# Dividing by the softmax sums behind the value product in the first three units of an attention and two-MLP kernel

## The chip, the cores and the metric

The kernel runs on one core of a Trainium2 chip. The metric is the device time of one execution in microseconds (us); the kernel before takes 991.06 us (median of three runs, 991.04 to 992.08). Engines are named as in the profile: PE is the matrix engine (TensorE), PEld its weight loads, DVE the vector engine, ACT the scalar engine, POOL is GpSimd, SP issues most transfers.

## What is computed

Three stages follow one another. The change is in the first; the inputs are 64-bit floats in memory, and the kernel works in 32-bit floats, with operands of large products split into a high and a low part (`xh`, `xl`).

```python
# attention: 4 batches, 8 heads, 576 positions, 64 wide, window of 128
scores = scale * q @ k.T                      # per batch and head
scores = where(mask, scores + bias, -1e9)     # ALiBi slope per head, causal window
attn = exp(scores - max(scores))
attn = attn / (sum(attn) + 1e-9)
x = attn @ v                                  # -> 2304 tokens x 512
# gated MLP
y = (silu(x @ w_gate) * (x @ w_val)) @ w_out
# second MLP
h = y @ w_in
out = (h * cos(h)) @ w_out2
```

## The kernel before

Attention works in 16 **units** `u`: a batch and a pair of heads, `NP` = 4 pairs to a batch, so units 0 to 3 are batch 0. A unit has nine **items** `(u, h, i)`: for each head four blocks of 128 rows (`i < NB`), and one tail item (`i == NB`) with the last 64 rows of both heads. Items go in groups of two, and the tail is a group by itself. The groups are called g0 (head 0, blocks 0 and 1), g2 (head 1, blocks 0 and 1), g4 and g6 (blocks 2 and 3 of the two heads) and the tail here.

A loop at line 635 makes one **step** for each item, and each engine's queue holds what the steps issued, in that order; nothing is reordered later. For a group the stages are: scores on PE into one of two `s` banks (`do_s`, issued two groups ahead), bias and row minimum on DVE (`do_bias`, L478), exponential with row sum on ACT (`do_exp`, L487), guard and reciprocal of the sums on DVE (`do_guard` L493, `do_recip` L498), the division on POOL (`do_norm`, L511), transposes on PE (`do_t`, L530; `folded` units 4 and later L520), a copy of the transposed block to SBUF on ACT (`do_hi`, L548, for the tail L543), and, once per unit, the product with the values on PE (`do_pv`, L584, for the tail L562 and L564). The end of `do_pv` is put off to the next step: ACT copies the high part (`xh`, L589, tail L571), DVE subtracts for the low part (`xl`, L590, tail L573). `staged` says how many steps behind a group its transposes, copies and value product come: 5, 6 and 8 (tail 9) in most units, 4, 5 and 6 in the last pair of a batch.

Beside this the loop prepares the next unit's queries and keys (`prep_t` on PE L407, `prep_q` on DVE L413, `prep_k` on ACT L416), and converts nine **pieces** of the first weights (`convert`): two ACT operations (L126, L128), three on DVE (L129, L136, L137), an addition (on POOL L146 for even pieces, on DVE L141 for odd ones), a high part (ACT L168 for even, POOL L173 for odd pieces) and a low part (POOL L161). The tail's value product takes the bank `pq` that the next unit's query transposes use, except in unit 3 of a batch (bank `pm`).

When a batch's last tail has ended (`release`), `filler` may run: dense matmuls of the first MLP (L81 to L83) between the attention's steps. Before batch 0 is through there is none.

Of the kernel before, what the change touches and what calls it, by code (L numbers as in the profile page):

```python
# [9 lines left out]
F32 = mybir.dt.float32  # L10
# [18 lines left out]
def kernel(  # L29
# [12 lines left out]
    nc = tc.nc  # L42
# [56 lines left out]

    def convert(dst, todo, fast=False, act=False):  # L100
# [13 lines left out]
        for i, (key, src, f, column, pool) in enumerate(todo):  # L114
# [19 lines left out]
            if wide:  # L134
# [5 lines left out]
                if fast or (act and i % 2):  # L140
                    nc.vector.tensor_tensor(out=ti, in0=ti, in1=r, op=ALU.add)  # L141
                    added.add(i)
                    yield
                else:
                    def add(i=i, ti=ti, r=r):
                        nc.gpsimd.tensor_tensor(out=ti, in0=ti, in1=r, op=ALU.add)  # L146
                        added.add(i)
                    pool_bg.append((1.25, add))
# [21 lines left out]
            if act and i % 2 == 0:  # L170
# [230 lines left out]
    ptt = const.tile([128, 256], F32, name="ptt")  # L401
    QT, KT, PQ = {}, {}, {}
# [42 lines left out]

    def do_s(groups):
# [3 lines left out]
        for g in groups:  # L450
# [4 lines left out]
            for m, n in enumerate(g):  # L455
# [10 lines left out]
                ST[n] = st, m  # L466
# [5 lines left out]
    def do_bias(n):  # L472
# [4 lines left out]
        st, m = ST[n]  # L477
# [6 lines left out]
    def do_exp(n):  # L484
        w = width(items[n][2])
        e, (st, m) = E[n], ST[n]
        nc.scalar.activation(out=e[:, :w], in_=e[:, :w], func=AF.Exp, bias=st[:, m:m + 1], scale=-1.0,  # L487
                             accum_out=st[:, 2 + 2 * m:3 + 2 * m])

    def do_guard(g):  # L490
        st = ST[g[0]][0]
        c = 2 * len(g) - 1
        nc.vector.tensor_scalar(st[:, 5:5 + c], st[:, 2:2 + c], 1e-9, None, ALU.add)  # L493

    def do_recip(g):
        st = ST[g[0]][0]
        c = 2 * len(g) - 1
# [7 lines left out]
    def do_norm(n):  # L505
        w = width(items[n][2])
        (st, m), e = ST.pop(n), E[n]
# [46 lines left out]

    def do_pv(n):
        u, h, i = items[n]
        b_, p = divmod(u, NP)
        if i == NB:
            vt = nat["v", u]
            ps = (pm.tile([128, 512], F32, tag="pm", name="pm") if u == NP - 1 else  # L560
# [26 lines left out]
        def fin():  # L587
            tok = slice(b_ * S, b_ * S + NB * 128)
            nc.scalar.copy(out=xh[:, p, tok], in_=ps)  # L589
# [36 lines left out]
    def last_pair(n):  # L626

        return 0 <= n < N and items[n][0] == NP - 1

    def staged(n, late, early):  # L630

        if last_pair(n - early) and n - early in final:
            return final[n - early]
        return None if last_pair(n - late) else final.get(n - late)
    for n in range(N + PVS + 2):
# [11 lines left out]
        turned, high = staged(n, TRANS, 4), staged(n, HIGH, 5)  # L647
# [22 lines left out]
        for back in (PVS + 1, PVS, PVS - 2):  # L670
            for m in (ended(back) or ())[-1:]:
                u_, h_, i_ = items[m]
                if (h_ == 1 and i_ == NB - 1 or i_ == NB) and back == (
                        PVS - 2 if last_pair(m) else PVS if i_ == NB - 1 else PVS + 1):
                    do_pv(m)
# [567 lines left out]
```

## Time and profile before

| | |
|---|---|
| median of three runs | 991.06 us |
| the profiled execution's own time | 991.6 us |
| its span, first to last instruction | 989.9 us |
| PE busy | 966.7 us, 98% of the span |
| DVE, ACT, POOL busy | 738.8, 594.0, 479.5 us |
| first bias (L478) of units 0, 1, 2, 3, 4 | 10.34, 21.99, 34.42, 46.99, 60.68 us |
| first filler matmul (L81) | 69.60 us |

[...] A table by form gives a line's instructions of one shape with count, sum and mean, and the idle time before them. A timeline row gives start, length, engine, line and operation, and in brackets the idle time before it with what ended it.

### The profile page before, as it was taken

Reading aid. Unit: us, or ns where it says so; the run is one execution under the profiler, and the core shown is the slowest. Engines: PE = TensorE matmul, PEld = TensorE weight load, DVE = VectorE, ACT = ScalarE, POOL = GpSimd, SP = SyncE. Lnnn points to the kernel's source line nnn. Section 1 sums busy time; section 2 is a strip of 40 time slices with the busy share of each in tenths; the row PEclk is TensorE's granted clock in tenths of the full one; section 3 lists DMA queues with packets and bytes.
Section 4 is the critical chain, followed back from the end, with each engine's and each line's share of the span. In section 5 each row is a group of like instructions: output and inputs, shape, how many; then the busy total and the mean of one; then the engine's idle time right before and its main releaser. Section 6 shows DMA issues by size and latency. Waiting matters only on the chain.

```text
span 989.9 us, 17035 instructions
## 1 busy us (share of the span) xinstructions
PE 966.7 (98%) x5616; PEld 885.2 (89%) x5616; DVE 738.8 (75%) x1552; ACT 594.0 (60%) x1365; POOL 479.5 (48%) x563
## 2 busy tenths in 40 slices
PE   6789999999999999999999999999999999999998
PEld 4468888889999999999999999888989898898886
DVE  6867777766288989989989755889666796666664
ACT  6976666643254545555455433877677776776663
POOL 5756556642245767769678720344222442223221
PEclk9979999999999999999999999999999999999999
DMA  7541333322373637547557625765667656576552
GB/s 181 157 111 45 97 95 74 73 59 91 112 277 107 203 128 235 191 139 249 166 172 243 198 87 167 285 200 185 241 200 230 198 164 198 187 241 201 160 179 85
DMA packets 145159, 163.65 MB, mean 165 GB/s; under 512 B 64688, under 2 KB 105648, under 8 KB 144816
## 3 DMA queue, kind: packets, MB, share of 16 engines
q1 hardware_dynamic: 143872, 162.27, 52.2%
q8 instruction: 45, 0.74, 0.3%
q10 hardware_dynamic: 1200, 0.30, 0.1%
q14 instruction: 42, 0.34, 0.1%
HBM read 126.88 MB, written 35.65 MB: 164 GB/s over the span
## 4 chain that ended last, share of the span: by engine, by line
PE 89%; DVE 3%; ACT 2%; DMA 2%; issue 2%; POOL 1%; SPq 0%; POOLq 0%; DVEq 0%; ACTq 0%
PE l L81 13%; PE l L83 13%; PE l L82 13%; PE pm L81 8%; PE pm L83 8%; PE pm L82 8%; PE pm L966 6%; PE pm L968 5%; PE pm L967 5%; PE s L470 4%; PE pv L584 3%; PE pq L407 1%; PE t L530 1%; PE t L520 1%; POOL e L511 1%
## 5 line engine op out<-in xcount | busy, mean ns | idle before, releaser
L1091 POOL TENSOR_TENSOR r<-r,c 128x384 f32<-128x384 f32 x96 | 104.4, 1089 | 261.7 <-ACT r L1089 172.9
L81 PE MATMUL pm<-xh,wh 128*128 128x384 f32 (+1 forms) x452 | 151.7, 336 | 0.2 <-DVE fu L254 0.2
L83 PE MATMUL pm<-xh,wl 128*128 128x384 f32 (+1 forms) x452 | 144.8, 320 | 0.0
L82 PE MATMUL pm<-xl,wh 128*128 128x384 f32 (+1 forms) x452 | 144.7, 320 | 0.0
L81 PE MATMUL l<-wo,hh 128*128 128x512 f32 x288 | 113.9, 395 | 0.0
L82 PE MATMUL l<-wo,hh 128*128 128x512 f32 x288 | 113.5, 394 | 0.0
L83 PE MATMUL l<-wo,hl 128*128 128x512 f32 x288 | 113.5, 394 | 0.0
L966 PE MATMUL pm<-xh,ws 128*128 128x384 f32 x318 | 107.7, 339 | 0.5 <-ACT q L1117 0.5
L787 POOL TENSOR_TENSOR cs<-cs,st 128x512 uint32<-128x512 uint32 x56 | 80.6, 1439 | 56.5 <-DVE cs L785 47.1
L968 PE MATMUL pm<-xh,ws 128*128 128x384 f32 x318 | 107.6, 338 | 0.0
L967 PE MATMUL pm<-xl,ws 128*128 128x384 f32 x318 | 107.1, 337 | 0.0
L511 POOL TENSOR_SCALAR e<-e,st 128x128 f32<-128x128 f32 (+1 forms) x144 | 60.9, 426 | 58.5 <-DVE st L498 43.7
L81 PEld LDWEIGHTS pm<-xh,wh 128*128 128x128 f32 x452 | 85.1, 188 | 4.0 <-issue 3.0
L82 PEld LDWEIGHTS pm<-xl,wh 128*128 128x128 f32 x452 | 85.3, 189 | 0.0
L83 PEld LDWEIGHTS pm<-xh,wl 128*128 128x128 f32 x452 | 85.0, 188 | 0.0
L1081 ACT ACTIVATE a<-c 128x384 f32<-128x384 f32 x96 | 49.7, 518 | 54.5 <-DVE c L1107 54.5
L487 ACT ACTIVATE e<-e,st 128x256 f32<-128x256 f32 (+1 forms) x144 | 68.0, 474 | 19.0 <-DVE st L478 13.6
L1086 DVE SCALAR_TENSOR_TENSOR r<-a,r 128x384 f32<-128x384 f32 x96 | 76.0, 792 | 3.3
L1088 ACT ACTIVATE r<-r 128x384 f32<-128x384 f32 x96 | 50.3, 524 | 42.7 <-DVE r L1086 42.7
L81 PE MATMUL l<-uh,wh 128*128 128x384 f32 x216 | 72.8, 337 | 0.1
L83 PE MATMUL l<-uh,wl 128*128 128x384 f32 x216 | 72.6, 336 | 0.0
L82 PE MATMUL l<-ul,wh 128*128 128x384 f32 x216 | 72.5, 336 | 0.0
(178 smaller groups left out, 2618.3 us busy)
## 6 DMA issues: line engine op xcount, KB each, us to landing
ws<-wid SPq DMA_DIRECT2D x168, 256.0 KB, 2.8
wo<-wod SPq DMA_DIRECT2D x48, 512.0 KB, 4.9
st<-in_moe_w_out_dram SPq DMA_DIRECT2D x28, 512.0 KB, 3.7
st<-in_moe_w_in_dram SPq DMA_DIRECT2D x16, 512.0 KB, 3.7
st<-in_moe_w_gate_dram SPq DMA_DIRECT2D x12, 512.0 KB, 4.0
st<-in_moe_w_val_dram SPq DMA_DIRECT2D x12, 512.0 KB, 4.0
wid<-sh SPq DMA_DIRECT2D x24, 256.0 KB, 4.2
wid<-sl SPq DMA_DIRECT2D x24, 256.0 KB, 4.0
```

Source lines behind the costliest of these rows:

```text
L81: nc.tensor.matmul(out=ps, lhsT=ah, rhs=bh, start=start, stop=False)
L82: nc.tensor.matmul(out=ps, lhsT=ah, rhs=bl, start=False, stop=False)
L83: nc.tensor.matmul(out=ps, lhsT=al, rhs=bh, start=False, stop=stop)
L487: nc.scalar.activation(out=e[:, :w], in_=e[:, :w], func=AF.Exp, bias=st[:, m:m + 1], scale=-1.0, accum_out=st[:, 2 + 2 * m:3 + 2 * m])
L511: nc.gpsimd.tensor_scalar(e[:, :w], e[:, :w], st[:, 8 + 2 * m:9 + 2 * m], 1.0, ALU.mult, ALU.mult)
L787: nc.gpsimd.tensor_tensor(out=ti, in0=ti, in1=st[:, :, 0], op=ALU.add)
L966: nc.tensor.matmul(out=o, lhsT=wh, rhs=xh_, start=start and kk == 0, stop=False, skip_group_check=True)
L967: nc.tensor.matmul(out=o, lhsT=wh, rhs=xl_, start=False, stop=False, skip_group_check=True)
L968: nc.tensor.matmul(out=o, lhsT=wl, rhs=xh_, start=False, stop=kk == 1, skip_group_check=True)
L1086: nc.vector.scalar_tensor_tensor(out=r, in0=a, scalar=-C2, in1=r, op0=ALU.mult, op1=ALU.add)
L1088: nc.scalar.activation(out=r, in_=r, func=AF.Abs)
L1091: nc.gpsimd.tensor_tensor(out=r, in0=r, in1=h, op=ALU.mult)
```

## The change

In units 0 to 2 the eight row-block items are no longer divided before their transposes (`late`). Their sums are gathered in one tile per unit (`ustats`); after g6 DVE adds the guard and takes the reciprocals once for all eight columns. PE transposes the eight columns into a row tile (`do_row`), DVE copies it to SBUF (`rt`), and PE spreads it over 128 partitions by four products with a constant 0/1 tile (`do_spread`, `pick`). After the value product DVE copies the spread reciprocals to SBUF and multiplies the product by them; POOL then makes the high and the low part. `pick` is set up by two more POOL operations at the start.

The steps behind a group become 3, 4 and 5 in units 0 to 2 (tail 4, 5 and 6), and 4, 5 and 6 in unit 3 (`lag`). The tail's value product of units 0 to 3 takes bank `pm`. For pieces 0 to 5 of the weights, POOL makes all additions and all high parts (`POOLED`).

```diff
+    POOLED = 6
-                if fast or (act and i % 2):
+                if fast or (act and i % 2 and i >= POOLED):
                     nc.vector.tensor_tensor(out=ti, in0=ti, in1=r, op=ALU.add)
-            if act and i % 2 == 0:
+            if act and i % 2 == 0 and i >= POOLED:
                 pool_bg.append((0.0, lambda high=high: post.append(high)))
+    def late(n):
+        u, _, i = items[n]
+        return u < NP - 1 and i < NB
-                ST[n] = st, m
+                ST[n] = (ustats[u], h * NB + i, 8 + h * NB + i) if late(n) else (st, m, 2 + 2 * m)
     def do_guard(g):
         st = ST[g[0]][0]
+        if late(g[0]):
+            if items[g[-1]][1:] == (1, NB - 1):
+                nc.vector.tensor_scalar(st[:, 16:24], st[:, 8:16], 1e-9, None, ALU.add)
+            return
     def do_recip(g):
+        if late(g[0]):
+            if items[g[-1]][1:] == (1, NB - 1):
+                nc.vector.reciprocal(out=st[:, 24:32], in_=st[:, 16:24])
+            return
     def do_norm(n):
+        if late(n):
+            return
+    def do_row(u):
+        RB[u] = pm.tile([128, 512], F32, tag="pm", name="pm")
+        nc.tensor.transpose(RB[u][0:8, 0:128], ustats[u][:, 24:32], ident)
+        post.append(lambda: nc.vector.tensor_copy(out=rt, in_=RB[u][0:8, 0:128]))
+    def do_spread(u):
+        for i in range(NB):
+            nc.tensor.matmul(out=RB[u][:, i * 128:(i + 1) * 128], lhsT=pick[:, i].rearrange("s x c -> s (x c)"),
+                             rhs=rt, start=True, stop=True)
     def do_pv(n):
-            ps = (pm.tile([128, 512], F32, tag="pm", name="pm") if u == NP - 1 else
+            ps = (pm.tile([128, 512], F32, tag="pm", name="pm") if u < NP else
         def fin():
+            if late(n):
+                x = fill_p.tile([128, F0, HT], F32, tag="fu", name="fu").rearrange("p f t -> p (f t)")[:, :NB * 128]
+                by = fill_p.tile([128, F0, HT], F32R, tag="fh", name="fh").rearrange("p f t -> p (f t)")[:, :NB * 128]
+                nc.vector.tensor_copy(out=f32(by), in_=RB.pop(u))
+                nc.vector.tensor_tensor(out=x, in0=ps, in1=f32(by), op=ALU.mult)
+                pool_bg.append((0.6, lambda: nc.gpsimd.tensor_scalar(xh[:, p, tok], x, 1.0, 0.0, ALU.mult, ALU.add)))
+                pool_bg.append((1.25, lambda: nc.gpsimd.tensor_tensor(
+                    out=xl[:, p, tok], in0=x, in1=f32(xh[:, p, tok]), op=ALU.subtract)))
+                return
+    def lag(n):
+        u, _, i = items[n]
+        if u < NP - 1:
+            return (3, 4, 5) if i < NB else (4, 5, 6)
+        return (4, 5, 6) if u == NP - 1 else (TRANS, HIGH, PVS + (i == NB))
```

How the queues stand then is shown at three places. The first is PE, from the first scores of unit 2 (`s<-kx,qx`) on; `t` are transposes, `pv` the value product of unit 1, `pq` the transposes of unit 3's queries. Before:

```order
L470 MATMUL s<-kx,qx 128x128 x2
L470 MATMUL s<-kx,qx 128x256 x2
L530 MATMUL t<-ident,e 128x128 x4
L407 MATMUL pq<-ident,q 128x128 x4
L530 MATMUL t<-ident,e 128x128 x4
L470 MATMUL s<-kx,qx 128x256 x4
L530 MATMUL t<-ident,e 128x128 x2
L419 MATMUL t<-ident,qkt 128x128
L407 MATMUL pq<-ident,k 128x128 x4
L530 MATMUL t<-ident,e 128x128 x3
L584 MATMUL pv<-pth_485,v 64x256
```

The same place in the changed kernel:

```order
L483 MATMUL s<-kx,qx 128x128 x2
L483 MATMUL s<-kx,qx 128x256 x2
L553 MATMUL t<-ident,e 128x128 x4
L583 MATMUL pm<-ident,us_202 8x128
L415 MATMUL pq<-ident,q 128x128 x4
L553 MATMUL t<-ident,e 128x128 x2
L588 MATMUL pm<-rt,pick 128x128 x4
L620 MATMUL pv<-pth_456,v 64x256
...
L483 MATMUL s<-kx,qx 128x256 x4
L553 MATMUL t<-ident,e 128x128 x3
```

The tail's transposes (`x2`), the spread and the whole value product of the unit before now stand ahead of the scores of g4 and g6 (`128x256 x4`) and of the first transposes of the new unit (`x3`).

The second place is DVE, in unit 1, from the bias of the last group but the tail to the tail (before: g6 on; after: the end of g4 on). `xl<-..., xh 64x64` is the low part of the tail of unit 0. Before:

```order
L478 ISA e,st_166<-s,rel 128x256
L478 ISA st_166 128x1
L493 TENSOR_SCALAR st_173<-st_173 128x3
L498 RECIPROCAL st_173<-st_173 128x3
L478 ISA e,st_167<-s,relt,slope 128x192
L478 ISA st_167 128x1
L590 TENSOR_TENSOR xl<-pv,xh 128x512
L129 TENSOR_SCALAR ct<-ct 128x512
L493 TENSOR_SCALAR st_166<-st_166 128x3
L498 RECIPROCAL st_166<-st_166 128x3
L573 TENSOR_TENSOR xl<-pq,xh 64x64 x2
L136 TENSOR_SCALAR ct<-ct 128x512
```

In the changed kernel:

```order
L491 ISA e,us_202<-s,rel 128x256
L491 ISA us_202 128x1
L609 TENSOR_TENSOR xl<-pm,xh 64x64 x2
L131 TENSOR_SCALAR ct<-ct 128x512
L491 ISA e,us_202<-s,rel 128x256
L491 ISA us_202 128x1
...
L138 TENSOR_SCALAR ct<-ct 128x512
L139 SCALAR_TENSOR_TENSOR ct<-st,ct 128x512
L491 ISA e,st_167<-s,relt,slope 128x192
L491 ISA st_167 128x1
L507 TENSOR_SCALAR us_202<-us_202 128x8
L516 RECIPROCAL us_202<-us_202 128x8
```

The tail's low part stood behind the biases of g6 and of the tail; it now stands ahead of both, and two operations of a weight piece (L138, L139) stand between them.

The third place is POOL in unit 3, from the division of g4 (`x2`) to that of the tail (`128x192`). Before:

```order
L511 TENSOR_SCALAR e<-e,st_167 128x256 x2
L173 TENSOR_SCALAR wh<-ct 128x512
L161 TENSOR_TENSOR wl<-ct,wh 128x512
L511 TENSOR_SCALAR e<-e,st_168 128x256 x2
L511 TENSOR_SCALAR e<-e,st_169 128x192
L146 TENSOR_TENSOR ct<-ct,st 128x512
```

In the changed kernel, from the parts of unit 2's product on:

```order
L630 TENSOR_SCALAR xh<-fu 128x512
L631 TENSOR_TENSOR xl<-fu,xh 128x512
L534 TENSOR_SCALAR e<-e,st_167 128x256 x2
L148 TENSOR_TENSOR ct<-ct,st 128x512
L534 TENSOR_SCALAR e<-e,st_168 128x256 x2
L534 TENSOR_SCALAR e<-e,st_169 128x192
```

The addition of the last piece (L148) has moved from behind the last divisions of batch 0 to a place ahead of two of them.

## Rows read from the trace of the kernel before

**Rows 1.** Windows: units 1, 2, 3, batch 0's end, and a stretch behind it.

```profile
21.99:34.42 12.43, 10.17 (x69) 6.51 (x67) 10.72 (x41) 11.32 (x35) 10.22 (x15) 1.00 0.53 136
34.42:46.99 12.57, 9.33 (x63) 6.03 (x63) 10.88 (x39) 11.41 (x35) 9.32 (x13) 1.00 0.64 171
46.99:60.68 13.69, 11.89 (x63) 7.91 (x63) 11.01 (x40) 11.40 (x35) 8.94 (x13) 0.75 0.48 122
60.68:69.57 8.89, 7.31 (x37) 4.44 (x37) 3.99 (x20) 4.18 (x14) 5.26 (x9) 0.62 0.21 48
80.00:90.00 10.00, 10.00 (x82) 8.78 (x82) 7.18 (x34) 6.28 (x24) 7.20 (x16) 1.00 0.21 47
```

**Rows 2.** Table by form, DVE in unit 2.

```profile
L493 DVE TENSOR_SCALAR st<-st 128x3 f32<-128x3 f32 x4 | 1.3, 317 | 0.5 <-ACT e L487 0.5
L129 DVE TENSOR_SCALAR ct<-ct 128x512 f32<-128x512 f32 x2 | 1.2, 592 | 0.0
L413 DVE TENSOR_SCALAR qx<-pq,qscale 128x512 f32<-128x512 f32 x1 | 0.7, 722 | 0.0
L498 DVE RECIPROCAL st<-st 128x3 f32<-128x3 f32 x4 | 0.7, 176 | 0.1
L590 DVE TENSOR_TENSOR xl<-pv,xh 128x512 fp32r<-128x512 f32 x1 | 0.7, 692 | 0.0
L141 DVE CUSTOM_DVE_ANT_0 ct<-st,ct 128x1024 uint16<-128x1024 uint16 x1 | 0.7, 659 | 0.0
```

**Rows 3.** The same table, ACT in unit 2.

```profile
L589 ACT CAST xh<-pv 128x512 fp32r<-128x512 f32 x1 | 0.6, 591 | 0.0
```

**Rows 4.** The same table, POOL in unit 2.

```profile
L511 POOL TENSOR_SCALAR e<-e,st 128x256 f32<-128x256 f32 x6 | 3.2, 547 | 0.5 <-DVE st L498 0.5
L161 POOL TENSOR_TENSOR wl<-ct,wh 128x512 fp32r<-128x512 f32 x2 | 2.5, 1274 | 0.7 <-ACT wh L168 0.6
L146 POOL TENSOR_TENSOR ct<-ct,st 128x512 uint32<-128x512 uint32 x1 | 1.3, 1298 | 0.0
L173 POOL TENSOR_SCALAR wh<-ct 128x512 fp32r<-128x512 f32 x1 | 0.8, 787 | 0.0
```

**Rows 5.** Timeline, PE: single groups of matmuls.

```profile
45.72 0.63 PE L407 MATMUL pq<-ident,q 128*128 128x128 f32 x4 [1.59 <-issue]
38.77 1.73 PE L584 MATMUL pv<-pth,v 128*64 128x256 f32 x16
62.88 2.08 PE L470 MATMUL s<-kx,qx 64*128 64x256 f32 x8
65.29 3.25 PE L584 MATMUL pv<-pth,v 128*64 128x256 f32 x16
```

**Rows 6.** Windows over runs of DVE's (first two) and ACT's work.

```profile
40.97:42.38 1.41, 0.96 (x7) 0.72 (x7) 1.38 (x10) 1.41 (x5) 0.93 (x3) 1.00 1.01 228
45.16:47.85 2.69, 1.36 (x9) 1.00 (x10) 2.54 (x11) 1.65 (x6) 1.26 (x3) 1.00 0.57 198
...
39.04:40.92 1.88, 1.88 (x18) 1.16 (x14) 1.85 (x7) 1.83 (x9) 1.47 (x2) 1.00 1.00 319
43.79:45.15 1.36, 0.34 (x4) 0.10 (x1) 0.35 (x2) 1.33 (x6) 1.28 (x2) 1.00 0.83 189
```

**Rows 7.** Timeline: a guard on DVE and a low part on POOL.

```profile
38.96 1.28 POOL L161 TENSOR_TENSOR wl<-ct,wh 128x512 fp32r<-128x512 f32 x1 [0.61 <-ACT wh L168]
39.49 0.77 DVE L493 TENSOR_SCALAR st<-st 128x3 f32<-128x3 f32 x1
```

**Rows 8.** Windows: three pauses of PE, and the stretch behind one.

```profile
31.50:35.10 3.60, 1.24 (x9) 0.84 (x8) 2.60 (x11) 2.53 (x9) 2.35 (x3) 1.00 0.72 199
44.20:47.90 3.70, 1.41 (x9) 1.05 (x10) 2.71 (x12) 2.63 (x10) 2.22 (x3) 1.00 0.60 186
48.00:54.70 6.70, 6.70 (x28) 4.24 (x28) 6.36 (x23) 6.34 (x20) 5.21 (x7) 0.50 0.59 156
57.90:61.60 3.70, 1.68 (x12) 0.96 (x10) 2.85 (x14) 2.65 (x11) 0.94 (x2) 1.00 0.75 170
```

More of the change, by code (lines that the diff above doesn't have):

```diff
@@ L401 @@
     ptt = const.tile([128, 256], F32, name="ptt")
+    ustats = [const.tile([128, 32], F32, name=f"us{j}") for j in range(NP - 1)]
+    rt = const.tile([8, 128], F32, name="rt")
+    pick = const.tile([8, NB, 2, 64], F32, name="pick")
+    nc.gpsimd.memset(pick, 0.0)
+    nc.gpsimd.affine_select(out=pick, in_=pick, pattern=[[-1, NB], [-NB, 2], [0, 64]], compare_op=ALU.not_equal,
+                            fill=1.0, base=0, channel_multiplier=1)
     QT, KT, PQ = {}, {}, {}
@@ L476, in do_bias @@
         e = e_p.tile([128, 256], F32, tag="e", name="e")
-        st, m = ST[n]
+        st, m, _ = ST[n]
         nc.vector.tensor_tensor_reduce(
@@ L485, in do_exp @@
         w = width(items[n][2])
-        e, (st, m) = E[n], ST[n]
+        e, (st, m, c) = E[n], ST[n]
         nc.scalar.activation(out=e[:, :w], in_=e[:, :w], func=AF.Exp, bias=st[:, m:m + 1], scale=-1.0,
-                             accum_out=st[:, 2 + 2 * m:3 + 2 * m])
+                             accum_out=st[:, c:c + 1])
     def do_guard(g):
         st = ST[g[0]][0]
+        if late(g[0]):
+            if items[g[-1]][1:] == (1, NB - 1):
+                nc.vector.tensor_scalar(st[:, 16:24], st[:, 8:16], 1e-9, None, ALU.add)
+            return
         c = 2 * len(g) - 1
@@ L506, in do_norm @@
         w = width(items[n][2])
-        (st, m), e = ST.pop(n), E[n]
+        (st, m, _), e = ST.pop(n), E[n]
+        if late(n):
+            return
         if folded(n) and w == 256:
@@ L553, in do_hi @@
                                     in1=mold, op=ALU.mult)
+    RB = {}
+    def do_row(u):
[6 more added lines that the diff above has]
+                             rhs=rt, start=True, stop=True)
     def do_pv(n):
@@ L624, with staged @@
     due = pdue = 0.0
[L626 to L634, printed above, removed]
+    def lag(n):
[3 more added lines that the diff above has]
+        return (4, 5, 6) if u == NP - 1 else (TRANS, HIGH, PVS + (i == NB))
+    def staged(n, stage):
+        for j in range(3, PVS + 2):
+            if n - j in final and lag(n - j)[stage] == j:
+                return final[n - j]
+        return None
     for n in range(N + PVS + 2):
@@ L646 @@
             do_s([first[u * NI + j] for j in AHEAD[idx]])
-        turned, high = staged(n, TRANS, 4), staged(n, HIGH, 5)
+        turned, high = staged(n, 0), staged(n, 1)
         if high:
@@ L669 @@
         due += 0.3 * RATE
[L670 to L675, printed above, removed]
+        valued = staged(n, 2)
+        if turned and items[turned[-1]][1:] == (1, NB - 1) and late(turned[-1]):
+            do_row(items[turned[-1]][0])
+        if valued and (items[valued[-1]][1:] == (1, NB - 1) or items[valued[-1]][2] == NB):
+            if late(valued[-1]):
+                do_spread(items[valued[-1]][0])
+            do_pv(valued[-1])
         if v1 is not None:
```

## The prediction

> **What bounds the kernel now.** I read the windows first [rows 1]. From about 70 us on PE is busy without a break (10.00 of 10 us from 80 to 90), so what happens there is fixed PE work, whose order the change leaves alone. Time can be won or lost only in batch 0, before the filler starts at 69.60 us; from then on every microsecond gained or lost goes straight to the end. Batch 0 runs in periods, one per unit: 12.43, 12.57 and 13.69 us for units 1 to 3, and 8.89 us from unit 4's first bias to the filler [rows 1]. In a period ACT works 11.3 to 11.4 us, DVE 10.7 to 11.0, POOL 8.9 to 10.2. No engine is full: ACT waits about 1 us for DVE's biases and DVE 1.5 to 2.7 us for ACT and PE. Two busy engines hand a chain to and fro, so the sums of work alone don't say what a period will be; the order of the queues counts as well.
>
> The second thing to see is PE's clock. It stands at 1.00 over units 1 and 2, at 0.75 on average over unit 3 and at 0.62 over the end [rows 1]. [...] Once low it stays so for 6.7 us of full PE work [rows 8]. The value product takes 3.25 us at the low level and 1.73 us at the high one, eight score matmuls 2.08 us at the low one, so some 1.04 at the high [rows 5].
>
> **The work, part by part, for each of units 0 to 2.** DVE loses three of its guards (0.32 us each), three reciprocals (0.18), one piece's addition (0.66) and the low part of the product (0.69): 2.85 us. It gains the copy of the spread reciprocals, which I price by the query copy, also from a PSUM bank and 512 wide (0.72), the product with them, priced by the low part, which reads the same two memories (0.69), and the row copy, for which I take a guard's 0.3: 1.7 us. Net -1.1 us [rows 2]. ACT loses the high part of the product (0.59) and one piece's high part, a cast of the same shape: -1.2 us [rows 3]. POOL loses eight divisions of about 0.55 us, 4.4 us, and gains 0.79 + 1.27 for the product's parts and 1.30 + 0.79 for a piece: 4.15 us [rows 4]; it stays as it is. PE gains four small products, like four query transposes (0.63), and one transpose of 8 columns, at most a quarter of that: 0.8 us [rows 5]. The wait of the query transposes for the tail's bank (1.59 us [rows 5]) goes away with the move to `pm`; but PE is not what a period waits for there, and I count nothing for it. The two set-up operations of `pick` run on POOL while the first inputs are still being loaded: nothing. By these sums a period would shrink by 1.1 to 1.2 us. That is the first rival. I don't forecast it, because of the order.
>
> **The loop of a period after the change.** I follow units 1 and 2 from DVE's low part of a tail around to the next one, in the queue order shown with the change. On DVE stand the tail's low part, a piece's L129 operation, the bias of g6, the piece's two others, the tail's bias, guard and reciprocal, the first bias of the next unit, and the tail's own guard and reciprocal. The rows of before hold the same operations in two runs, 1.41 and 2.69 us [rows 6], without the L129 one, 0.59 [rows 2]: 4.7 us. Then POOL divides the tail, 0.55 at most [rows 4]. Then PE, in order: the tail's transposes (0.4, from four in 0.63), the spread (0.63), the value product (1.73), the scores of g4 and g6 (1.04), the first transposes (0.5): 4.3 us [rows 5]. Only then can ACT copy the first transposed block, and its queue is in order too: behind that copy come the next queries' tail, a piece's L128 operation, the exponentials of g4, and only then the tail's high part, for which DVE's low part waits. The same operations take 1.88 and 1.36 us [rows 6]: 3.2 us. Sum 4.7 + 0.55 + 4.3 + 3.2 = 12.8 us. The work got less by 1.1 us, but the value product and the spread have come into the chain, and the tail's low part, which stood behind the biases of g6 and the tail, now holds both up. So a period is 12.8 us in place of 12.43 and 12.57: +0.6 us for units 1 and 2 together. Bounds: -1.1 each (the sums), +1.0 each.
>
> [...] A guard on three elements took 0.77 us where others take far less, and it ended within 0.02 us of the end of POOL's low part beside it [rows 7]. [...]
>
> **The start.** Up to unit 1's first bias DVE loses three guards and three reciprocals, 1.5 us at the means, and the addition of piece 1, 0.66 [rows 2]: 2.1 us at most. The piece's next operations still wait for their load and for ACT, so I take -1.6. Bounds: 0 and -2.1.
>
> **The clock.** At the end of unit 1 the score matmuls of unit 2 need the bank that the bias of g6 frees, and then the one that the tail's bias frees. Between these stand two DVE operations of a piece, and ahead of the first stands the wait for ACT. In my walk PE has, between the tail's scores and the second of these banks, 4.4 us with only the transposes of g4 (0.63) and one or two score matmuls, about 0.8 us of work. That is a longer and emptier pause than the two behind which the clock fell and the one behind which it did not [rows 8]. So I expect a fall to 0.50 there, near 32 us, which the kernel before doesn't have. It hits the PE part of the loop, which is now in the chain: at the low level throughout, its 4.3 us become 8.2, +3.9; if PE is low only in front of the value product, +1.3. I take +2.6 for unit 2. Bounds: 0 and +3.9.
>
> **Unit 3 and the end.** Unit 3 keeps its divisions on POOL, and ran with the low clock before as well [rows 8]. DVE gets the row copy, the copy and the multiplication of unit 2 for one low part: +1.0 us by the prices above, and I take +0.9. Bounds: -1.1 (no fall there: 13.69 becomes unit 2's 12.57 [rows 1]) and +2.5. Behind it the last piece's addition, 1.30 us [rows 4], now stands on POOL ahead of the divisions of g6 and the tail; the tail's transposes wait for these, and the whole end waits for the transposes: +1.3. Bounds: 0, and if the clock stays up here the scores and the value product give back 2.6 us [rows 5].
>
> **Sum.** -1.6 + 0.6 + 2.6 + 0.9 + 1.3 = +3.8 us. Against the profiled execution's own 991.6 us that is 995.4; the median of the runs, 991.06, is 0.5 us lower, and I predict against it: 994.9 us.
>
> **Rivals.** 1. *The work decides*: ACT and DVE each lose 1.1 to 1.2 us in three units, and the queues shift so that the waits stay as they are: -3.3 us, 987.8. For it: both stand at 11 of 12.5 us [rows 1]. Against it: the loop above has the same length with less work in it. Chance 0.18. [...] Chance 0.10. 3. *It falls only where it falls now*: -1.6 + 0.6 + 0.9 + 1.3 = +1.2 us, 992.3; speaks for it that one pause in three passed without a fall [rows 8]. Chance 0.25. 4. The *forecast*, a new fall in unit 2: 0.47.
>
> **Range and chances.** 0.2% of this kernel is 2 us, about what its measurement can tell from no change. Rivals 1 and 2 are faster by more than that (0.28), rival 3 and the mild edge of the forecast lie within it (0.28), the rest is slower (0.44). The forecast with its clock terms at the upper bounds gives -1.6 + 0.6 + 3.9 + 2.5 + 1.3 = +6.7, 997.8. The range runs from 988.0, which leaves out the better part of rival 1, to 998.0. The forecast's own range is 992.5 to 998.0.
>
> **What would show it.** In the changed kernel's windows: unit 1's first bias near 20.4 us; periods near 12.8 us, with ACT near 10.2 and DVE near 10 us of work in them; PE's granted clock at 0.50 somewhere between 31 and 42 us; DVE's low part of the tail waiting 2 us for ACT's cast; ACT's first copy of a unit waiting 1 to 2 us for PE; POOL's division of the last g6 behind an addition. If DVE never waits long at the tail's low part, the loop is wrong and rival 1 holds. [...] If the filler starts before 68 us the forecast has failed.

## The result and the profile after

The changed kernel takes 1003.54 us (median of four runs, 1001.54 to 1003.78) against 991.57 us for the kernel before beside it: a ratio of 1.0114, 95% interval 1.0101 to 1.0127, so about 12 us slower. Forecast were 994.9 us with a range up to 998.0. The direction was right, the size was not.

The windows view of the changed kernel, for units 1, 2, 3 and the end of batch 0. These lines answer [rows 1] and have the same columns: the stretch and its length, the busy time of PE, PEld, DVE, ACT and POOL with the number of instructions, the granted clock of PE as a share of its full one, the transfer share and GB/s.

```profile
21.35:37.26 15.91, 11.47 (x71) 7.83 (x69) 10.53 (x35) 11.44 (x37) 10.45 (x10) 0.84 0.43 111
37.26:54.72 17.46, 14.01 (x73) 9.98 (x72) 11.34 (x36) 9.69 (x32) 8.67 (x9) 0.70 0.52 128
54.72:72.52 17.80, 13.97 (x70) 9.68 (x70) 11.20 (x40) 10.13 (x33) 9.00 (x13) 0.69 0.45 111
72.52:81.99 9.47, 9.12 (x49) 6.09 (x50) 4.61 (x20) 5.11 (x17) 5.10 (x11) 0.61 0.01 2
```

The filler begins at 81.99 us in place of 69.60, 12.39 us later, and the span grows from 989.9 to 1002.0 us: all of the loss lies in batch 0, and the dense part behind it is as long as before. Unit 1's first bias comes 0.64 us earlier than before (21.35 against 21.99). Then units 1, 2 and 3 lose 3.5, 4.9 and 4.1 us and the end 0.6 us. ACT's work in unit 2 fell from 11.4 to 9.7 us, and its period grew from 12.6 to 17.5 us: the work was taken away and the waiting more than took its place.

The granted clock differs as well. The same view over the stretches in which it was low, and over two of the pauses in front of them:

```profile
25.40:28.60 3.20, 3.20 (x20) 1.97 (x16) 1.48 (x3) 0.00 (x0) 1.93 (x2) 0.50 0.55 162
32.97:35.60 2.63, 0.46 (x2) 0.29 (x2) 2.52 (x10) 2.63 (x8) 0.27 (x1) 0.98 1.04 291
35.70:45.80 10.10, 9.80 (x43) 7.02 (x45) 7.28 (x21) 5.04 (x16) 6.78 (x7) 0.50 0.61 160
50.62:53.07 2.45, 0.00 (x2) 0.03 (x1) 2.34 (x9) 1.27 (x4) 0.82 (x1) 0.89 0.00 1
52.70:62.70 10.00, 9.60 (x43) 6.69 (x43) 6.97 (x25) 6.93 (x21) 5.20 (x7) 0.50 0.45 113
69.80:79.90 10.10, 9.33 (x37) 6.00 (x39) 5.47 (x27) 5.17 (x18) 6.12 (x11) 0.50 0.14 31
```

Before batch 0 is through, PE is at the low level (0.50) for some 34 us. In the kernel before it was low from 48 to 54.8 us [rows 8] and from 61.6 to 68.4 us, some 13.6 us:

```profile
61.70:68.40 6.70, 6.14 (x27) 3.35 (x27) 2.64 (x13) 2.53 (x9) 5.26 (x9) 0.50 0.14 32
```

So two of the four falls, at 25.2 and 35.4 us, are new. The other two, at 52.5 and 69.6 us, stand at the seams where the kernel before had its falls, behind unit 2 and behind unit 3, but the clock now stays low for 10.2 us in place of 6.8. In the first of the four stretches ACT does nothing at all (0.00 us of work): it waits for PE.

One round, from the tail's low part in unit 1 to that in unit 2, in the timeline of the changed kernel:

```profile
32.82 0.46 DVE L609 TENSOR_TENSOR xl<-pm,xh 64x64 fp32r<-64x64 f32 x2 [3.05 <-ACT xh L607]
35.74 1.29 POOL L148 TENSOR_TENSOR ct<-ct,st 128x512 uint32<-128x512 uint32 x1 [2.50 <-ACT e L500]
35.86 1.20 DVE L507 TENSOR_SCALAR us<-us 128x8 f32<-128x8 f32 x1
38.37 0.42 POOL L534 TENSOR_SCALAR e<-e,st 128x192 f32<-128x192 f32 x1 [1.34 <-DVE st L519]
39.55 0.63 PE L553 MATMUL t<-ident,e 128*128 128x128 f32 x2
40.11 2.07 PE L588 MATMUL pm<-rt,pick 8*128 8x128 f32 x8
42.11 3.25 PE L620 MATMUL pv<-pth,v 128*64 128x256 f32 x16
45.30 1.32 PE L483 MATMUL s<-kx,qx 64*128 64x256 f32 x8
47.24 0.48 ACT L571 COPY pth<-t 128x384 f32<-128x384 f32 x1 [4.06 <-PE t L427]
50.47 0.46 DVE L609 TENSOR_TENSOR xl<-pm,xh 64x64 fp32r<-64x64 f32 x2 [2.02 <-ACT xh L607]
```

These are the links of the prediction's chain: the tail's low part on DVE (L609, 32.82), the division of the tail on POOL (38.37), the transposes, the spread (L588), the value product (L620) and the scores on PE, the first copy on ACT (47.24, after 4.06 us of waiting), and the next low part (50.47). The round takes 17.65 us where the walk had 12.8. The value product runs at the low clock, 3.25 us, as in the last line of [rows 5].

### The profile page after: what moved, and what is told of

It is laid out like the page before. It is cut to its first block, busy times and chain, and to the rows that moved or that the text cites. A ratio compares the mean times of both kernels' runs of the same rounds, so it can differ in the third digit from the quotient of the medians.

```text
span 1002.0 us, 17052 instructions
## 1 busy us (share of the span) xinstructions
PE 974.9 (97%) x5643; PEld 893.7 (89%) x5643; DVE 736.4 (73%) x1537; ACT 591.2 (59%) x1359; POOL 477.8 (48%) x553
## 4 chain that ended last, share of the span: by engine, by line
PE 88%; DVE 4%; ACT 3%; DMA 2%; issue 1%; POOL 1%; SPq 0%; ACTq 0%; DVEq 0%; POOLq 0%
PE l L81 13%; PE l L83 13%; PE l L82 12%; PE pm L81 7%; PE pm L83 7%; PE pm L82 7%; PE pm L1016 5%; PE pm L1018 5%; PE pm L1017 5%; PE s L483 4%; PE pv L620 3%; PE pq L415 1%; PE t L553 1%; PE t L543 1%; DMA st<-in_moe_w_val_dram 1%
## 5 line engine op out<-in xcount | busy, mean ns | idle before, releaser
L534 POOL TENSOR_SCALAR e<-e,st 128x128 f32<-128x128 f32 (+2 forms) x120 | 46.8, 392 | 63.8 <-DVE st L519 35.9
L1016 PEld LDWEIGHTS pm<-xh,ws 128*128 128x128 f32 x318 | 59.8, 188 | 8.4 <-ACT q L1167 1.0
```

What stands on the lines that cost most here:

```text
L534: nc.gpsimd.tensor_scalar(e[:, :w], e[:, :w], st[:, 8 + 2 * m:9 + 2 * m], 1.0, ALU.mult, ALU.mult)
L1016: nc.tensor.matmul(out=o, lhsT=wh, rhs=xh_, start=start and kk == 0, stop=False, skip_group_check=True)
```

## The experiments

All differ from the changed kernel by the lines shown, unless it is said otherwise.

### The clock, and each part undone alone

First, PE's pauses were filled with small matmuls that nobody reads, so that the clock stays up while the order and the work of the other engines stay the same.

```diff
+    def warm(k, new=False):
+        if new:
+            WM[0] = pm.tile([128, 512], F32, tag="pm", name="pm")
+        for _ in range(k):
+            nc.tensor.matmul(out=WM[0][:, :128], lhsT=ident, rhs=rel[:, :128], start=True, stop=True)
...
+        if idx == 0 and 1 <= u <= NP:
+            warm(5)
...
+        if idx == NI - 1 and u < NP:
+            warm(3, True)
+        if idx == 3 and 1 <= u < NP:
+            warm(2)
...
+                if j == 0 and x == 1 and 1 <= items[groups[0][0]][0] <= NP and items[groups[0][0]][2] == 0:
+                    warm(3)
```

> The changed kernel with 8 small matmuls of constants (128 columns each, no reader) in PE's pauses at the start of units 1 to 4, 3 ahead of the last transposes of units 0 to 3 and 2 ahead of the tail's transposes of units 0 to 2. Theory 1, the low clock on the chain: the changed kernel runs PE at 0.50 for about 34 us before the filler (25.2 to 28.6, 35.5 to 45.7, 52.5 to 62.8, 69.6 to 79.8 us); filled, the clock stays at 1.00 over most of that, and the time falls by 8 us or more, to 989 to 995 us. Theory 2, the longer loop itself, whatever the clock: the time stays above 999 us even where the clock stays up.

Measured: 996.0 us, ratio 1.0044 (1.0027 to 1.0061), between the two expectations. That is 7.5 us below the changed kernel, and still 4.4 us above the kernel before. Its windows over units 1, 2, 3 and the end of batch 0:

```profile
22.12:37.09 14.97, 13.32 (x102) 10.51 (x102) 11.20 (x35) 11.46 (x35) 10.59 (x10) 1.00 0.41 113
37.09:51.35 14.26, 12.34 (x97) 9.74 (x95) 10.38 (x37) 10.26 (x32) 9.23 (x9) 1.00 0.64 164
51.35:67.17 15.82, 13.38 (x96) 10.20 (x96) 11.22 (x40) 9.72 (x32) 9.74 (x15) 0.94 0.50 122
67.17:74.75 7.58, 6.72 (x50) 5.21 (x50) 4.61 (x20) 5.05 (x17) 4.37 (x10) 0.89 0.01 2
```

The clock is at 1.00 through units 1 and 2, and the periods are 15.0 and 14.3 us in place of 15.9 and 17.5. Stretch by stretch, against the changed kernel, the fills gave back 0.9, 3.2, 2.0 and 1.9 us, and the start came 0.8 us later. So the low clock is a large part of the loss, and the rounds are still longer than 12.8 us at the full clock.

Three runs undo one part each. The old lags:

```diff
-        if u < NP - 1:
-            return (3, 4, 5) if i < NB else (4, 5, 6)
         return (4, 5, 6) if u == NP - 1 else (TRANS, HIGH, PVS + (i == NB))
```

> The changed kernel with the lags of before (5, 6 and 8, tail 9) in units 0 to 2; the division stays behind the value product. Theory 1 and theory 2 both take the short lags as what put the spread and the value product ahead of the scores of g4 and g6, and the tail's low part ahead of the bias of g6: with the old lags the work lost decides, and the time is 986 to 992 us. Theory 3, the later division itself costs (its spread at 1.15 us, its copy and its multiplication on DVE): 997 us or more.

Measured: 992.75 us, 1.0009 (0.9999 to 1.0018), just above the range for the work alone. 10.8 us of the 12 are gone, so the short lags, not the later division, carry the loss; but the gain that the work alone would give isn't there either. Its windows for units 1 and 2 show the clock low here too: it stands at 0.84 in unit 1 and at 0.76 in unit 2, in place of the 1.00 of [rows 1].

```profile
21.17:34.21 13.04, 11.87 (x78) 9.13 (x78) 11.47 (x36) 11.50 (x35) 9.79 (x10) 0.84 0.49 132
34.21:48.28 14.07, 12.38 (x72) 9.01 (x70) 10.78 (x35) 9.44 (x30) 7.93 (x9) 0.76 0.52 138
```

The weight pieces back where they were:

```diff
-    POOLED = 6
+    POOLED = 0
```

> The changed kernel with the weight pieces' additions and high parts back on DVE and ACT for odd and even pieces (POOLED = 0). Theories 1 and 2: within 2 us of the changed kernel, 1001 to 1006 us, since POOL is not what the loop waits for. Theory 4, the shift of the pieces to POOL is what delays the end: 998 us or less.

Measured: 998.95 us, 1.0074 (1.0058 to 1.009), 4.6 us below the changed kernel, between the two expectations and nearer to theory 4. The shift of the pieces to POOL, which the prediction priced at no loss, costs more than a third of the whole.

The division back on POOL, with the short lags and the shifted pieces kept:

```diff
     def late(n):
-        u, _, i = items[n]
-        return u < NP - 1 and i < NB
+        return False
```

> The changed kernel with the divisions of units 0 to 2 back on POOL ahead of the transposes (no row, no spread, no multiplication; the product's parts by ACT and DVE as before), the short lags and the pieces on POOL kept. If the short lags alone make the loop long and the clock low: 999 to 1008 us. If the spread and the work behind the product are the cause: 994 us or less.

Measured: 1001.39 us, 1.0095 (1.008 to 1.011): the loss is there without any spread, row or late multiplication. The short lags and the shifted pieces are enough for it.

### The pieces on POOL, at the full clock

c2 is c1 with `POOLED = 0`.

> The changed kernel with the same small matmuls in PE's pauses as c1_fill_pauses, and the weight pieces back on DVE and ACT as before (POOLED = 0). c1 took 996.0 us at a clock of 1.00, u2 998.95 us at the low one. If the pieces' place on POOL costs by itself, through DVE's stretched guard and the addition ahead of the last divisions, and not through the clock: 992 to 994 us. If it cost only because the clock was low: 995 us or more, as c1.

Measured: 990.93 us, 0.9997 (0.9987 to 1.0006), below both expectations. With the pauses filled (7.5 us) and the pieces back (5.1 us) the changed kernel is as fast as the kernel before. But filling the pauses makes the kernel before faster too, by 2.6 us (w1, below). Like for like, the loss of 12 us is some 5 us of additional low clock, 5 us of pieces, and 1.8 us (990.93 against w1's 989.12) that stay with both undone. c2's windows and one round:

```profile
21.96:35.12 13.16, 12.96 (x102) 10.50 (x103) 10.96 (x37) 10.96 (x36) 7.53 (x7) 1.00 0.62 166
35.12:48.26 13.14, 12.57 (x100) 10.14 (x98) 11.30 (x36) 10.84 (x34) 7.53 (x7) 1.00 0.56 147
48.26:63.55 15.29, 13.14 (x98) 9.82 (x95) 13.63 (x42) 10.81 (x33) 11.45 (x15) 1.00 0.54 133
63.55:69.60 6.05, 5.39 (x44) 3.85 (x44) 3.77 (x21) 4.48 (x16) 5.25 (x9) 1.00 0.02 4
```

```profile
31.11 0.46 DVE L611 TENSOR_TENSOR xl<-pm,xh 64x64 fp32r<-64x64 f32 x2 [0.61 <-ACT xh L609]
36.22 0.43 POOL L536 TENSOR_SCALAR e<-e,st 128x192 f32<-128x192 f32 x1 [2.64 <-DVE rt L586]
36.70 0.44 PE L555 MATMUL t<-ident,e 128*128 128x128 f32 x2 [0.42 <-POOL e L536]
37.07 1.15 PE L590 MATMUL pm<-rt,pick 8*128 8x128 f32 x8
38.15 1.73 PE L622 MATMUL pv<-pth,v 128*64 128x256 f32 x16
41.57 0.48 ACT L573 COPY pth<-t 128x384 f32<-128x384 f32 x1 [2.01 <-PE t L427]
44.26 0.46 DVE L611 TENSOR_TENSOR xl<-pm,xh 64x64 fp32r<-64x64 f32 x2 [0.61 <-ACT xh L609]
```

The round takes 13.15 us, near the 12.8 of the walk, and every hand-over in these lines is waited for: POOL 2.64 us for DVE, PE 0.42 for POOL, ACT 2.01 for PE, DVE 0.61 for ACT. So the chain of the prediction is tight once the clock is up; that it alone sets the period is not shown, and c5 below speaks against it. In c1 the round reads, in the same view:

```profile
32.13 0.46 DVE L611 TENSOR_TENSOR xl<-pm,xh 64x64 fp32r<-64x64 f32 x2 [3.08 <-ACT xh L609]
35.62 1.29 POOL L148 TENSOR_TENSOR ct<-ct,st 128x512 uint32<-128x512 uint32 x1 [2.29 <-ACT e L502]
35.73 1.20 DVE L509 TENSOR_SCALAR us<-us 128x8 f32<-128x8 f32 x1
38.15 0.43 POOL L536 TENSOR_SCALAR e<-e,st 128x192 f32<-128x192 f32 x1 [1.24 <-ACT pth L573]
38.63 0.44 PE L555 MATMUL t<-ident,e 128*128 128x128 f32 x2 [0.23 <-POOL e L536]
43.50 0.48 ACT L573 COPY pth<-t 128x384 f32<-128x384 f32 x1 [1.14 <-PE t L427]
44.75 0.68 ACT L130 ACTIVATE st<-st 128x512 uint32<-128x512 uint32 x1
46.76 0.46 DVE L611 TENSOR_TENSOR xl<-pm,xh 64x64 fp32r<-64x64 f32 x2 [2.16 <-ACT xh L609]
```

Leg by leg, from these lines and those of the changed kernel (DVE: from its low part to POOL's division; POOL: to PE's transposes of the tail; PE: to ACT's first copy; ACT: to the next low part):

| | DVE | POOL | PE | ACT | round |
|---|---|---|---|---|---|
| forecast | 4.7 | 0.55 | 4.3 | 3.2 | 12.8 |
| c2: clock up, pieces back | 5.11 | 0.48 | 4.87 | 2.69 | 13.15 |
| c1: clock up, pieces on POOL | 6.02 | 0.48 | 4.87 | 3.26 | 14.63 |
| changed kernel | 5.55 | 1.18 | 7.69 | 3.23 | 17.65 |

With the pieces on POOL, DVE's guard L509 takes 1.20 us beside POOL's addition, in c2 0.16 to 0.17; and a piece's ACT operation L130, 0.68 us, stands in ACT's leg, where the prediction had one too and c2 has none. The stretched guard is no feature of every round: in units 0 and 2 it takes 0.17 us in the changed kernel and in c1. And c2's DVE leg has a stretched operation of its own, the piece's L131 at 32.67 us, 1.20 us long where its shortest takes 0.41; in c1 it takes 0.99 at the same place. By the windows, c1 loses 1.8 and 1.1 us against c2 in units 1 and 2, and 2.1 us in unit 3 and the end together (23.40 against 21.34), where its clock was not quite up.

Which half of the shift is it? c3 has only the odd pieces' additions back on DVE, c4 only the even pieces' high parts back on ACT.

```diff
-                if fast or (act and i % 2 and i >= POOLED):
+                if fast or (act and i % 2):
...
-            if act and i % 2 == 0 and i >= POOLED:
+            if act and i % 2 == 0:
```

(The first pair of lines is c3, the second c4; both on top of c1.)

> As c1_fill_pauses (pauses filled, clock 1.00, 996.0 us), with only the odd pieces' additions back on DVE; the even pieces' high parts stay on POOL. c2, with both back, took 990.9 us. If the additions on POOL (1.29 us each, beside DVE's guard that stretches to 1.20 us, and ahead of the last divisions) cost the 5 us: 991 to 992.5 us. If the high parts on POOL cost them: 994.5 us or more.

> As c1_fill_pauses, with only the even pieces' high parts back on ACT; the odd pieces' additions stay on POOL. The other half of the same question: 994.5 us or more if the additions cost the 5 us, 991 to 992.5 us if the high parts do.

Measured: 990.7 us (0.9985, 0.9976 to 0.9995) and 991.45 us (1.0, 0.9991 to 1.001). Each run alone would put the cost on the half that it takes back, so the expectations fail together: either half alone costs next to nothing, and only both together cost 5 us. Units 1 and 2 take 13.06 and 13.03 us in c3, 12.78 and 12.95 us in c4, and unit 3 and the end together 21.35 and 21.63 us, near c2's 21.34. With both halves on POOL the pieces' steps come to stand at other places of DVE's and ACT's queues, in unit 1 with L130 and the stretched guard inside the round. That this is what makes the 1.8 and 1.1 us is argued from the rows, not shown by a run of its own; in unit 2 the guard isn't stretched, and its 1.1 us stay open.

### Moving one operation of the round

Four kernels cut the round at one link and keep the rest. v1 puts the spread and the value product one step later, behind the scores:

```diff
-            return (3, 4, 5) if i < NB else (4, 5, 6)
+            return (3, 4, 6) if i < NB else (4, 5, 6)
```

> The changed kernel with the spread and the value product of units 0 to 2 one step later (lags 3, 4, 6; tail as it was), so that PE takes them behind the scores of g4 and g6 and the new unit's first transposes. Theory A, one loop of tail low part (DVE), tail division (POOL), spread, value product and scores (PE), first copy to tail's high part (ACT): a good part of PE's leg (8.45 us of a 17.6 us round at the low clock) leaves it, the rounds fall to 13 to 14.5 us, the time to 992 to 997 us. Theory B, the short lags of the transposes and copies alone: 1000 us or more.

Measured: 1000.57 us, 1.0086 (1.0061 to 1.0112). Theory A's range failed; the time is where theory B put it. In the timeline the long PE work, moved, holds up others:

```profile
44.20 2.07 PE L588 MATMUL pm<-rt,pick 8*128 8x128 f32 x8
44.31 0.48 ACT L571 COPY pth<-t 128x384 f32<-128x384 f32 x1 [1.92 <-PE t L427]
46.20 3.25 PE L620 MATMUL pv<-pth,v 128*64 128x256 f32 x16
46.31 0.69 DVE L628 COPY fh<-pm 128x512 f32<-128x512 f32 x1 [3.11 <-PE pm L588]
50.65 0.43 ACT L607 CAST xh<-pm 64x64 fp32r<-64x64 f32 x2 [3.44 <-PE pm L600]
```

ACT's first copy waits 1.92 us in place of 4.06, but then ACT's cast waits 3.44 us for the tail's value product, which stands behind the spread and the product, and DVE waits 3.11 us for the spread. Unit 2 takes 19.41 us, at a mean clock of 0.59.

v2 puts the tail's high and low part one step later (the lines shown), v4 two steps (with one more `post.append` around it):

```diff
-            post.append(fin)
+            post.append((lambda: post.append(fin)) if u < NP - 1 else fin)
```

> The changed kernel with the tail's high and low part of units 0 to 2 one step later, so that DVE's low part stands behind the bias of g6 in place of ahead of it; PE's order is untouched. Theory A: the same loop is cut at its other end, since the bias of g6 no longer waits for ACT's cast; rounds of 13 to 15 us, 992 to 998 us. If PE's order (spread and value product ahead of the scores) costs by itself, without the tail's low part: 1000 us or more.

> The changed kernel with the tail's high and low part of units 0 to 2 two steps later, so that DVE's low part stands behind the biases of g6 and of the tail, as in the kernel before. In v2_tail_later it still stood ahead of the tail's bias and the round stayed at 15.7 to 17 us. Theory A, the round through the tail's low part: now cut, rounds of 13 to 15 us, 992 to 997 us. If the low clock and PE's order make the round without the tail's low part: 998 us or more.

Measured: 998.84 us (1.0073, 1.0047 to 1.01) and 1000.36 us (1.0095, 1.0079 to 1.0111), with unit 2 at 16.99 and 16.28 us. The first is only just above its range, the second well above. In both, PE is at the low clock for a third to three fifths of units 1 to 3 (mean clock 0.69 to 0.83), in unit 2 ACT's first copy waits 4.96 and 3.92 us for it, and the low part waits 1.83 and 1.73 us for ACT's cast. In v4:

```profile
48.15 0.48 ACT L571 COPY pth<-t 128x384 f32<-128x384 f32 x1 [3.92 <-PE t L427]
53.24 0.46 DVE L609 TENSOR_TENSOR xl<-pm,xh 64x64 fp32r<-64x64 f32 x2 [1.73 <-ACT xh L607]
```

The same move at the full clock, on top of c2:

> As c2_fill_no_pooled (clock 1.00, pieces as before, rounds of 13.15 us from one low part of the tail to the next), with the tail's high and low part two steps later, behind the biases of g6 and of the tail. At the low clock this move (v4) brought 3 us. If the round through the tail's low part is what sets the period at the high clock: rounds under 12.7 us and 987 to 990 us. If another chain of nearly the same length stands behind it: 990.5 us or more.

Measured: 994.77 us, 1.0028 (1.0016 to 1.004), 3.8 us worse than c2, as expected for another chain of nearly the same length behind the first. In unit 1, where the clock was at 1.00, the period grew from 13.16 to 14.02 us: the low part now waits for a later cast and stands in front of the guard and the next unit's first bias.

```profile
33.47 0.46 DVE L611 TENSOR_TENSOR xl<-pm,xh 64x64 fp32r<-64x64 f32 x2 [2.17 <-ACT xh L609]
```

PE, with its fills, is busy for all of that unit (14.02 of 14.02 us), so that the fills themselves hold it up is not ruled out. In unit 2 the fills no longer met the pauses, and the clock was low from about 38.2 to 45.0 us (0.54 on average from 38.05 to 45.5). In all these runs the move of one operation made the queues wait at another place and gave no gain at the full clock. No run took the tail's low part out of DVE's queue altogether; that is left open.

### What the later division is worth

If the clock decides so much, then it should also hold back the kernel before. In w1 its pauses, which lie elsewhere, got 5, 2, 3 and 5 small matmuls (`warm` as above, on the kernel before):

```diff
+        if idx == 4 and 1 <= u < NP:
+            warm(2)
...
+        if u == NP and idx in (2, 3):
+            warm(idx * 2 - 1)
...
             if idx == Q0:
+                if 1 <= u < NP:
+                    warm(5)
                 prep_t(v1, "q")
```

> The kernel before with small matmuls of constants (128 columns) in PE's pauses: 5 ahead of the query transposes of units 1 to 3, 2 ahead of the scores of g4 there, 3 and 5 ahead of the last two groups of transposes of batch 0. If the clock's low level costs the kernel before what its stretches show (13.69 us against 12.57 for unit 3, and 2.6 us at the end of the batch): PE at 1.00 up to the filler, 987 to 989.5 us. If the pauses, not the clock, set these stretches: within 1 us of the kernel before.

Measured: 989.12 us, 0.9973 (0.9964 to 0.9983): faster than the kernel before by 2.6 us, with no change of its work. The end gives it all: unit 4's first bias to the filler takes 6.03 us in place of 8.9, while units 1 and 2 grow by 0.3 us each and unit 3 stays as long as in [rows 1]. So by this run the low clock cost the kernel before nothing in unit 3.

```profile
47.61:61.27 13.66, 10.31 (x72) 6.81 (x71) 11.90 (x39) 11.34 (x35) 9.20 (x13) 1.00 0.59 158
61.27:67.30 6.03, 5.92 (x50) 4.47 (x49) 3.75 (x20) 4.18 (x14) 4.83 (x8) 1.00 0.26 58
```

The next ones have the later division with the old lags, and fills inside the pairs of score groups. In w2 they stand in two places of each pair:

> The changed kernel with the lags of before (5, 6, 8, tail 9) in units 0 to 2, and 4 or 5 such matmuls behind the first scores of each pair of groups in units 1 to 3. The unfilled one ran at the low clock from about 19 to 26, 38 to 45 and 51 to 54 us and took 992.75 us. If the clock is what keeps the later division from a gain there: 987 to 990 us. If not: 991.5 to 994 us.

Measured: 999.59 us, 1.0078 (1.0063 to 1.0094). PE has no pause left, and now the fills are what the scores wait for; of the clock it tells nothing.

```profile
24.16:39.17 15.01, 15.01 (x109) 11.71 (x110) 10.42 (x35) 10.90 (x34) 10.65 (x10) 1.00 0.51 130
```

w3 has them in one place, w4 the pieces back as well (`POOLED = 0`):

```diff
+        u, _, i = items[groups[0][0]]
+                if j == 0 and x == 1 and i < NB and (1 <= u < NP or u == NP and i == 0):
+                    warm(4 if i else 3, i == 0)
```

> As w2_old_lags_filled, with 3 or 4 small matmuls in one place of each pair of score groups in place of 4 or 5 in two places. In w2 PE was busy without a pause at a clock of 1.00 and the fills themselves delayed the scores. If the clock is what keeps the later division with the old lags (992.75 us) from a gain: 988 to 990.5 us. If not: 991.5 to 994 us.

> As w3, and the weight pieces back on DVE and ACT (POOLED = 0): the later division alone, at the old lags and with PE's pauses filled. If the shift of the pieces to POOL costs in the old order too: 1 to 3 us below w3. If POOL has room there and DVE and ACT don't: above w3.

Measured: 989.97 us (0.9986, 0.9976 to 0.9995) and 989.86 us (0.9975, 0.9965 to 0.9986). With the old lags the fills give back 2.8 us (992.75 to 989.97), and the shift of the pieces, worth 5 us with the short lags, is worth 0.1 us here. What is left over in w4 is the end of the batch, where the clock still fell:

```profile
59.55:68.90 9.35, 8.21 (x42) 5.14 (x43) 4.01 (x20) 4.21 (x14) 6.77 (x11) 0.63 0.18 41
```

w5 fills that place too; w6 is w5 with the division on POOL in all units.

```diff
+        if u == NP and idx in (2, 3):
+            warm(3, False)
         if turned:
             do_t(turned)
```

> As w4_old_lags_no_pooled_filled (old lags, pieces as before, division behind the value product in units 0 to 2, 989.9 us), with 3 small matmuls ahead of each of the last two groups of transposes of batch 0, where w4 still fell to the low clock at 61.5 us and needed 9.35 us from unit 4's first bias to the filler. With the clock up that stretch should take about 6.1 us, as in c2 and in the filled kernel before: filler near 65.7 us, 986 to 988 us, under the filled kernel before (989.1 us). If the clock falls elsewhere instead: 989 us or more.

> As w5, with the division back on POOL ahead of the transposes in all units: old lags, pieces as before, the tail's value product in the other bank, pauses filled. If the later division is worth something once the clock stays up (2.85 us of DVE's and 0.59 us of ACT's work less, 1.7 us more, in each of three units): 1 to 3 us above w5. If it is worth nothing: within 0.8 us of w5.

Measured: 987.84 us (0.9968, 0.9957 to 0.998) and 991.11 us (0.9994, 0.9984 to 1.0005). w5 is the fastest of all: by its ratio some 3.2 us under the kernel before, and 15.7 us under the changed kernel. The expected 1 to 3 us between w5 and w6 came out as 3.3; but the clock did not stay up in every execution of w6 (means of 0.993 to 0.999). Taking only executions with a mean clock of 0.998 or more, the medians are 987.77 (five of w5) and 990.15 us (six of w6): 2.4 us. So against the same order without it, the later division is worth about 2 to 3 us, near the 3.3 us of the prediction's first rival. But w6, which divides on POOL as the kernel before does, is itself 2 us slower than w1, the filled kernel before. Against w1, w5 is 0.5 us better by the ratios, with intervals that overlap; that the later division beats the filled kernel before is not shown.

## Why the prediction was wrong, step by step

Two terms of the sum failed: the pieces' shift, put at nothing but for the end's addition (+1.3 us), measured 5.1 us (c1 against c2), and the clock, put at +2.6 us for one new fall, measured 7.5 us (the changed kernel against c1), of which the kernel before loses 2.6 us as well (w1).

**The start** (-1.6 forecast): unit 0's period fell from 11.65 to 10.44 us, -1.2, but its first bias came 0.57 us later (10.91 against 10.34), so that unit 1 began 0.64 us earlier in place of 1.6: the first queries landed at 5.88 us in place of 5.31, and why they did no run shows. Within the bounds.

**The work** was priced nearly rightly where it could be seen. ACT had 9.7 us in unit 2 (forecast near 10.2), and 11.4 in unit 1, into whose longer window two more operations of a piece fell. DVE's work was 10.5 and 11.3 us in units 1 and 2, over the forecast's 10: some 0.6 us in each came back as operations that took longer than the shortest of their form (1.8 and 2.1 us in all, before 1.3 and 1.4), and unit 2 held one more step of a piece. One price was wrong: the spread was taken as four query transposes, 0.63 us. Its four products are recorded as x8 and take 1.15 us at the full clock and 2.07 at the low one (c2 and the changed kernel, above); four transposes are recorded as x4.

**The loop** (12.8 us) has the links, order and waits that were walked. But the walk was of the kernel with the pieces on POOL, and that round measured 14.63 us at the full clock (c1), 1.8 more: 1.3 in DVE's leg, of which the stretched guard is 1.0, and 0.6 in PE's, nearly all of it the spread. This is the first failed step. With the pieces back (c2) the round is 13.15 us; that it is so near 12.8 is partly luck, since there DVE's and PE's legs are 0.4 and 0.6 us longer than walked and ACT's 0.5 shorter. The prediction said of the pieces that POOL "stays as it is" and that DVE and ACT lose 0.66 us and a cast; it asked how much work moved, not where the pieces' other steps would stand in DVE's and ACT's queues afterwards. A stretched guard, of which [rows 7] has one, was not in the sum. It came, once: 1.20 us in unit 1, ending at 37.06, with POOL's addition ending at 37.03. In c2, c3 and c4 the same guard takes 0.16 to 0.17 us. That the operation beside it on POOL is what stretches it is the author's reading of the two ends; no run tried it by itself. Summed over batch 0 such stretches grew little: what DVE's instructions took beyond the shortest of their form is some 7.0 us before and 7.7 us after. One of them now lies in the round.

**The clock** (+2.6 in unit 2, bounds 0 to +3.9) is the second failed step. For unit 2 itself the price was near: the fills gave back 3.2 us there, and POOL's and PE's legs together, 8.75 us by the price for the low clock throughout, measured 8.87. (From its own rows the prediction's 8.2 for PE's leg would be 8.4, and the spread's true price adds 0.8; the leg measured 7.69, with the clock up again from 45.7 us, before its end.) But only one new fall was in the sum. Pauses of this kind stand at every seam between units, and the clock falls in or behind each: at 25.2, 35.4, 52.5 and 69.6 us, where the sum had the fall near 32 us and the two of the kernel before. The expectation "0.50 somewhere between 31 and 42 us" held, and told too little: a cause that repeats at each seam had to be priced at each, and the two old falls were not as cheap as before: the fills gave back 3.9 us in unit 3 and the end (c1), in the kernel before 2.6 (w1). Filling the pauses gave back 7.5 us in all. Rival 2 (chance 0.10), the clock that never falls, was put at 988.6 us; c1 measured 996.0, with one short fall left at 65.4 us. It lacked the 5 us of the pieces; with them back and the clock at 1.00 throughout (c2) the time is 990.9, with unit 3 (15.29 us, below) and the spread longer than forecast.

The length of a single wait of PE does not sort the falls. The fall at 25.2 us followed waits of 1.14 and 0.85 us, that at 38.2 us in c5 a single one of 1.41 us, and the clock stayed up behind one of 1.60 us in the kernel before (31.6 us). The falls at 52.5 and 69.6 us came within single waits of 2.45 and 3.39 us and tell less. What the runs show is the place: in the changed kernel the clock falls at every seam, four times. What decides it there, no run shows.

**Unit 3** (+0.9) lost 4.1 us. About half is the longer low stretch, 52.5 to 62.7 us against 48 to 54.8 before, with ACT waiting 4.1 us for PE at its end: c1 took 2.0 us less. With the clock at 1.00 and the pieces back (c2) unit 3 still took 15.29 us, 1.6 more than in the kernel before. The lower bound, 13.69 becoming 12.57 without the fall, is not borne out: w1 took 13.66 at a clock of 1.00. **The end** (+1.3) lost 0.6 us net. The addition ahead of the last divisions is there,

```profile
71.45 1.28 POOL L148 TENSOR_TENSOR ct<-ct,st 128x512 uint32<-128x512 uint32 x1
72.71 0.94 POOL L534 TENSOR_SCALAR e<-e,st 128x256 f32<-128x256 f32 x2
```

so the place was right. Its price was not measured by itself: in c2 to c4, where no addition stands ahead of these divisions, unit 3 and the end take 21.3 to 21.6 us, and in c1, where one does, 23.4 us, but there the clock fell as well.

**The chances.** The forecast's mechanism had 0.47, and it happened, with two new falls in place of one and the old two made longer; but it is not the whole loss. The range ended at 998.0, because the upper bounds were added for one new fall, and of the pieces only the end's 1.3 was in the sum. Had the fall been priced in units 1, 2 and 3 at the loop's own +3.9 us, the sum would have been -1.6 + 0.6 + 3 x 3.9 + 0.9 + 1.3 = +12.9 us; measured were +12.4 to the filler. That it fits so well would have been luck: the fills gave back 0.9, 3.2 and 2.0 us in these units, and the pieces' 5 us are not in the sum.

## What to carry to other kernels

When a change lengthens PE's pause at a seam that repeats, price the clock's fall at every seam (here four falls and some 34 us at 0.50), and price PE's work behind it at the low clock (the value product took 3.25 us in place of 1.73) as soon as other engines wait for it in order. An amount of work moved between engines says little while queues are in order: two shifts that cost nothing alone cost 5 us together, as the rows suggest by where their neighbours came to stand. Filling PE's pauses with matmuls that nobody reads is a cheap test of how much of a loss is the clock, and here a gain by itself: 2.6 us in the kernel before. The kernel that one compares with has to be filled too, and too many fills hold up the work, as in w2 (999.59 us).

## What the runs showed of the hardware

- The granted clock fell behind pauses whose longest single wait was 1.14 us (25.2 us in the changed kernel) and 1.41 us (38.2 us in c5), and did not fall in c1 with a wait of 1.17 us between fills (34.6 us), in c4 behind one of 1.36 us (57.3 us), nor in the kernel before behind one of 1.60 us (31.6 us). So the longest wait alone does not tell.
- The same program gets different clocks from one execution to the next, and its time follows loosely: w6 took 988.98 us at a mean clock of 0.998 and 993.83 us at 0.993, but also 992.26 us at 0.998.
- Four products of 8 x 128 by 128 columns in 32 bits take 1.15 us at the full clock (c2), four transposes of 128 columns 0.60 to 0.63 us.
